# A planned order for a recurrent block beside full attention: transfers modelled alike, paired tails and products of values set beside the wide scores

## The chip, the cores and the metric

The kernel runs on one core of a Trainium2 chip. The time is the device time of one execution in microseconds (us), as a median of several executions. A core has five engines, each with its own instruction stream: PE multiplies matrices (its weight loads are listed apart as PEld), DVE and ACT work element by element and empty PE's accumulators (PSUM banks), POOL does small copies and issues transfers, and SP only issues transfers (DMA). Engines wait for one another through semaphores.

## The reference, cut to what matters

Two attention blocks read the same input `x` (2048 x 576); a gate per row mixes them.

```python
def _A_ref(x, mem0, Wq, Wk, Wv, Wo, seg_len):      # 32 heads of 128; seg_len 32, memory of 8 rows
    mem = mem0
    for s in range(n_seg):                         # 64 segments, one after the other
        h = jnp.concatenate([mem, xs], axis=1)     # 8 + 32 = 40 rows
        q, k, v = (jnp.einsum('btd,dhe->bhte', h, W) for W in (Wq, Wk, Wv))
        p = _softmax(jnp.where(mask, jnp.einsum('bhqe,bhke->bhqk', q, k) * scale, -1e9))
        o = jnp.einsum('bhte,hed->btd', jnp.einsum('bhqk,bhke->bhqe', p, v), Wo)
        mem = o[:, :M, :]                          # the memory of the next segment
        outs.append(o[:, M:, :])
def _B_ref(x, wqkv, wo):                           # plain attention, 32 heads of 18, 2048 x 2048 scores
    ...
g = _sigmoid((x * gate_w).sum(-1, keepdims=True))
return g * _A_ref(...) + (1 - g) * _B_ref(...)
```

Block A is a recurrence: segment s+1 cannot start before segment s has given its 8 memory rows. Block B has no such order, so its work can fill the time in which A waits.

## The kernel before, in words

All work is recorded as named operations (`add`, L148), each with an engine or a choice of two, a planned duration, its dependencies, a priority, buffers that it takes and gives back, and for transfers their size. `Plan.run` (L207) then places them one at a time: for every engine `choose` (L306) takes, among those that could start about first, the one with the lowest priority number, and the operation that can start earliest of all engines is placed. The result is a fixed order of instructions on each engine; on the chip each engine works through its list in that order and waits where an input is late. The planner's times are used for nothing else.

The operations that matter here, by name, segment s and half hf (16 heads each):

- `sb` (L925): one visit of block B, four concurrent matmuls of 32 rows by 128 columns ("the wide scores", mode `row`); `ex` and `ey` (ACT, L934 and L938): its exponentials; `ob` (L948): the product with the values, four matmuls of 128 rows by 32 columns (mode `col`). There are 512 visits. Scores `sb` have one buffer, exponentials `etb` two.
- `TQ0`, `TQ1`, `TV0` (L1302): the tails of two projections paired, eight matmuls of 64 by 32 (mode `quad`), three in each segment. `Q0`, `K0`, `Q1`, `K1`, `V0`, `V1` (L1312): the rest of the projections, four pieces each, mode `col`.
- `eQ`, `eK`, `eV`: copies out of PSUM (L520 on DVE, L518 on ACT); `t` (L1377): a transposing transfer on SP; `ct` (L1386): its copy into place on DVE; `ph` (L1401, L1409): A's scores; `xp`, `sm`, `rc`, `bc`, `nm`: the softmax; `po` (L1477): A's product of values, 16 matmuls of 64 by 128 (mode `tall`); `op` (L1183): the output projection; `fo` (L1525): memory rows for the next segment.
- `la` (L1018, L1022): projections of the last 8 rows of each segment, 24 units per group of 16 segments; group 0 must be ready before segment 0 can end, the others fill the recurrence. Their copies go through three buffers `vl` and are stored to `qkd` or `vld`.
- `warm` (L895): four matmuls on zeros that add nothing. The planner puts one where it foresees PE idle for more than 0.216 us, and only between the first and the last `ob` of a group of visits.

A visit may not start before a place in the recurrence has been reached (last lines of the kernel: from visit 48 on, 64 segments share the rest evenly). A planner's term `switch`, between 0.028 and 0.383, is added to the priority of any PE operation whose mode differs from the one before. `transfer` (L180) says when a transfer lands: it had one rule for the first 125 us by queue and another for later, and the weight loads of block A (`behind`, L649) were not modelled as transfers at all, only as time on POOL. `TURNS` is a table of numbers, one for each third of a segment, from which factors on the priorities of that stretch are drawn; it was found by search, offline.

Of the kernel before, what the change touches and what calls it, by code (L numbers as in the profile page):

```python
# [12 lines left out]
ACT = mybir.ActivationFunctionType  # L13
# [3 lines left out]

RANKS = [
    {
        "switch": 0.158, "near": 0.011, "early": 0.195, "wait": 0.273, "Q0": 0.964, "K0": 3.412, "Q1": 5.846,  # L20
# [5 lines left out]
        "cp": 0.432, "mn": 1.531,  # L26
    },
    {
        "switch": 0.383, "near": 0.014, "early": 0.178, "wait": 0.273, "Q0": 0.268, "K0": 3.152, "Q1": 5.787,
# [5 lines left out]
        "cp": 1.117, "mn": 1.531,  # L35
    },
    {
        "switch": 0.088, "near": 0.019, "early": 0.168, "wait": 0.273, "Q0": 0.05, "K0": 4.557, "Q1": 5.756,
# [5 lines left out]
        "mn": 1.531,  # L44
    },
    {
        "switch": 0.028, "near": 0.019, "early": 0.264, "wait": 0.014, "Q0": 0.05, "K0": 3.865, "Q1": 4.013,
# [7 lines left out]
]  # L55
RANK = dict(RANKS[0])
TURNS = [
# [16 lines left out]
]  # L74
FACTORS = (0.02, 0.1, 0.25, 0.4, 0.55, 0.7, 0.85, 1.0, 1.2, 1.5, 1.9, 2.4, 3.0, 4.0, 6.0, 10.0)
KNOBS = ("switch", "near", "early", "wait", "gap")


def mixed(turn, k):
# [35 lines left out]
class Plan:  # L115

    LANES = 8
    LATE = {"ACT": 0.055, "DVE": 0.055, "POOL": 0.06, "SP": 0.03}
    OWN = {"PE": 0.0, "ACT": 0.0, "DVE": 0.03, "POOL": 0.0, "SP": 0.0}
    OVER = {"PE": 0.0, "ACT": 0.1, "DVE": 0.08, "POOL": 0.0, "SP": 0.0}  # L120
    LAG = {"SP": 0.66, "ACT": 0.66, "POOL": 1.25}
    FAR, LANDED, RATE = 0.235, 0.025, 200.0
    EARLY = 125.0
    SWITCH = 0.103
    WARM = 0.216
    BLOCK, FETCH = 128, 3.8
    TURN = re.compile(r"(TQ0|ph0|op0)\.\d+(\.0)?$")
# [19 lines left out]

    def add(  # L148
        self, name, engs, dur, fn, deps=(), prio=5.0, mode=None, take=(), give=(), dmas=0, kb=0.0,
        pairs=4, alt=None, waits=0.0, drain=0.226, lag=None,  # L150
    ):
        op = Op(name, engs, dur, fn, deps, prio, mode, take, give)
        op.dmas, op.kb, op.lag = dmas, kb, lag
        op.pairs, op.alt, op.waits, op.drain = pairs, alt, waits, drain
        op.kind = self.kinds.setdefault(kind_of(name), len(self.kinds))
        op.seq = len(self.ops)
        self.ops.append(op)
        return op
# [21 lines left out]
    def transfer(self, op):  # L180
        step = (op.end - op.start) / op.dmas
        lag = self.LAG[op.eng] if op.lag is None else op.lag
        for j in range(op.dmas):
            issued = op.start + (j + 1) * step
            if op.end < self.EARLY and op.eng == "POOL":
                self.moved = max(self.moved, issued + 0.6) + op.kb / op.dmas / 290.0
                op.land = max(self.moved + 1.0, op.end + 2.2 + op.kb / 250.0)
            elif op.end < self.EARLY:
                self.moved = max(self.moved, issued + 0.6) + op.kb / op.dmas / 290.0
                op.land = self.moved + 0.5  # L190
            else:
                self.moved = max(self.moved, issued + lag) + op.kb / op.dmas / self.RATE
                op.land = self.moved + 0.55
            if op.eng != "POOL":
                self.lanes.append(max(op.land, self.lanes[-1]))
        self.lanes = self.lanes[-self.LANES:]
# [9 lines left out]
    def run(self):  # L206
# [96 lines left out]
                dirty = set(free)  # L303
        return order

    def choose(self, e, ops, now, mode):  # L306
        found = []
        for op in ops:
# [24 lines left out]

        def rank(f):
            op = f[1]
            switch = 0.0 if e != "PE" or mode in (op.mode, op.alt and op.alt[0]) else self.rank["switch"]
            return (self.weighed(op) + switch, op.seq)

        got = min(near, key=rank)
        urgent = [f for f in found if self.weighed(f[1]) < 1.0 and f[0] > got[0]]  # L340
        if urgent and self.weighed(got[1]) >= 1.0:
            u = min(urgent, key=lambda f: (f[0], f[1].seq))
# [19 lines left out]
def kernel(  # L362
# [286 lines left out]
    def behind(name, beat, corner, n, fn, deps, kb):  # L649

        mark = add(f"mk{name}", "DVE", 0.07, lambda e: nc.vector.memset(corner(), 0.0), [beat, *deps], prio=0.05)
        op = add(name, "POOL", 0.6 * n, fn, [mark, *deps], prio=0.15, kb=kb)
        paced.append(op)
        return op

# [577 lines left out]
    for s in range(n_seg):  # L1233
# [39 lines left out]
                        in_=xl[:, f, a, :, :].rearrange("p u (h t) -> p u h t", t=LO),  # L1273
                    )

        pl = add(f"pl{s}", "POOL", 0.95, put_l, [ll, prev.get("psh0"), prev.get("psh1")], prio=1.0, give=(("xl", ll, 0),) if s % 4 == 3 else ())

        def ld_v(e, s=s):
            for jj in range(2):
# [81 lines left out]
        for hf, ev in ((0, ev0), (1, ev1)):  # L1361
            before = [ev, prev.get(f"pso{hf}")]
            pvs.append((
                add(f"qv{hf}.{s}", "SP", 1.17, put_v(hf), before, prio=0.2, dmas=2, kb=64),
                add(f"qc{hf}.{s}", ("DVE", "POOL"), (0.585, 1.3), put_v(hf), before, prio=RANK["qc"]),
            ))

# [2 lines left out]
        for hf in range(2):  # L1370
# [3 lines left out]
            for a, ev_a in ((0, eq), (1, ek)):  # L1374
                def turn(e, hf=hf, s=s, a=a):
                    box["tt", s, a, hf] = tt = given(opened["fix"], "tt", [P, 4, P], BF16)
                    nc.sync.dma_start_transpose(out=tt[:, :, :], in_=box["tm", s, "QK"[a] + str(hf)][:, :])  # L1377

                t_ = add(
                    f"t{a}{hf}.{s}", "SP", 1.21, turn, [ev_a], prio=RANK[f"t{hf}"], take=("tt",),  # L1380
                    give=(("tm", ev_a, 0),), dmas=1, kb=128, lag=0.02,
                )

                def ct(e, hf=hf, s=s, a=a):
                    eng = nc.vector if e == "DVE" else nc.gpsimd
                    eng.tensor_copy(  # L1386
                        out=opened["qk"][:, hf, a, 0:16 * L].rearrange("p (j i t) -> p j i t", i=4, t=L)[:, :, :, 0:CT],
                        in_=box["tt", s, a, hf][:, :, :].rearrange("p i (j t) -> p j i t", t=CT),
                    )

                turned.append(add(
                    f"ct{a}{hf}.{s}", "DVE", 0.3, ct, [t_, prev.get(f"psh{hf}")],
                    prio=RANK["ct"], give=(("tt", t_, 0),),
                ))
# [380 lines left out]
```

## Time and profile before

| | us |
|---|---|
| median of 3 executions | 1467.12 (1464.38 to 1468.97) |
| the profiled execution, and its span | 1468.2, 1466.3 |
| tails of segment 0, 1 and 63 start | 129.6, 185.4, 1416.9 |
| PE busy in the span | 1346.6 |
| ACT, DVE, POOL busy | 1130.2, 785.0, 565.2 |

The span falls into three stages. In the start (to 185.4 us, where segment 1 begins) block B's projections, the first visits, the loading of A's weights and the first `la` group are done. In the recurrence (to 1416.9) segments follow at mostly 18 to 22 us each with visits in between. The tail is the last segment and the mix. A row of the timeline gives the start, the length, the engine, the line and the operation; matmuls overlap in the pipeline, so what a piece costs PE is the distance from its start to the next start, not its length.

### The profile page before, as it was taken

To read this page: it belongs to the slowest core of one execution; us is meant where nothing else is said; L and a number is where in the kernel's file an instruction comes from. 1 tells how busy PE (TensorE), PEld (TensorE's weight loads), DVE (VectorE), ACT (ScalarE), POOL (GpSimd) and SP (SyncE) were. 2 spreads that over 40 slices of the span, in tenths; PEclk is the share of its full clock that TensorE was granted. 3 is DMA by queue.
4 is the path that set the end of the run, shared out by engine and by line. 5 is a ranking of instruction groups with operands and counts; after the bars stand their busy time and mean duration, and the time that the engine had idled before them with its cause. 6 is when DMAs were issued, how large, how long until landed. Compare 5 with 4: busy or idle time off the path is not lost.

```text
span 1466.3 us, 73309 instructions
## 1 busy us (share of the span) xinstructions
PE 1346.6 (92%) x32558; PEld 685.0 (47%) x32558; DVE 785.0 (54%) x1892; ACT 1130.2 (77%) x1367; POOL 565.2 (39%) x1221
## 2 busy tenths in 40 slices
PE   8778899999999999999999999999998988899998
PEld 5335344455544444444554444555444434444445
DVE  5233465555555555545655545556555555555556
ACT  3455598888887888877888888887777877887885
POOL 8233235233542435313542316443244334442420
PEclk9899999999999999999999999999999999999999
DMA  8787434232432233232333333323234222422225
GB/s 244 217 286 244 132 65 93 56 66 54 86 65 61 55 71 87 59 69 53 84 71 71 52 71 66 84 59 79 55 73 93 52 58 48 79 55 59 50 59 185
DMA packets 245080, 130.64 MB, mean 89 GB/s; under 512 B 197583, under 2 KB 231111, under 8 KB 244763
## 3 DMA queue, kind: packets, MB, share of 16 engines
q1 hardware_dynamic: 216067, 80.47, 24.5%
q0 software_dynamic: 26560, 43.31, 11.1%
q8 instruction: 254, 4.16, 1.2%
q10 hardware_dynamic: 2136, 2.19, 0.5%
q14 instruction: 63, 0.52, 0.1%
HBM read 52.74 MB, written 31.12 MB: 57 GB/s over the span
## 4 chain that ended last, share of the span: by engine, by line
PE 58%; DMA 25%; DVE 9%; ACT 4%; issue 3%; SPq 1%; DVEq 0%; ACTq 0%; POOL 0%
DMA tt<-tm 17%; PE pvv L1312 15%; PE acc L1183 10%; PE sb L925 7%; PE ob L948 5%; PE pv L1018 4%; DVE tm L520 3%; PE pvv L1302 3%; PE pso L1477 2%; ACT etb L934 2%; DMA v_sb<-tm 2%; DMA qkd<-vl 2%; PE pq L727 2%; DMA ktd<-xn 2%; PE pv L1022 2%
## 5 line engine op out<-in xcount | busy, mean ns | idle before, releaser
L934 ACT ACTIVATE etb<-sb 128x1536 bf16<-128x1536 f32 x512 | 743.9, 1453 | 210.3 <-PE sp L925 124.2
L520 DVE CAST tm<-pvv 128x512 bf16<-128x512 f32 x336 | 230.8, 689 | 217.2 <-PE pvv L1312 203.1
L938 ACT ACTIVATE etb<-sp 128x512 bf16<-128x512 f32 x512 | 305.4, 596 | 2.8 <-PE sp L925 2.7
L1312 PEld LDWEIGHTS <-ht 128*32 128x32 bf16 x6144 | 141.1, 96 | 168.9 <-issue 74.3
L925 PE MATMUL sp<-qch,kch 32*128 32x512 bf16 x512 | 197.6, 386 | 14.6 <-DVE vl L520 5.0
L948 PE MATMUL ob<-etb,vch 128*32 128x512 bf16 x2048 | 201.3, 386 | 5.9 <-DMA vch<-vgd 5.7
L925 PE MATMUL sb<-qch,kch 32*128 32x512 bf16 x1536 | 202.2, 388 | 4.8 <-ACT etb L934 3.9
L1183 PE MATMUL acc<-wo,ot 128*32 128x288 bf16 (+1 forms) x6144 | 167.2, 250 | 5.0 <-issue 2.7
L1312 PE MATMUL pvv<-wk_m,ht 128*32 128x512 bf16 x2048 | 148.6, 382 | 0.0
L1386 DVE COPY qk<-tt 128x512 bf16<-128x512 bf16 x256 | 81.0, 320 | 126.2 <-DMA tt<-tm 124.6
L1312 PE MATMUL pvv<-wq_m,ht 128*32 128x512 bf16 x2048 | 141.7, 381 | 0.4 <-issue 0.4
L1312 PE MATMUL pvv<-wv_m,ht 128*32 128x512 bf16 x2048 | 141.0, 381 | 0.0
L1183 PEld LDWEIGHTS <-ot 128*32 128x32 bf16 x6144 | 116.3, 97 | 37.8 <-issue 16.0
L925 PEld LDWEIGHTS <-kch 32*128 32x128 bf16 x2048 | 54.1, 91 | 145.4 <-issue 136.7
L1354 POOL COPY v_sb<-tm 32x512 bf16<-32x512 bf16 x90 | 56.6, 629 | 167.1 <-DVE tm L520 139.8
L520 DVE CAST ot<-pso 128x320 bf16<-128x320 f32 x158 | 73.7, 488 | 72.7 <-PE pso L1477 69.5
L1252 POOL COPY ht<-xg 128x120 bf16<-128x120 bf16 x64 | 19.5, 305 | 207.0 <-PE pvv L1312 190.8
L1419 ACT ACTIVATE et<-psh 128x320 bf16<-128x320 f32 x128 | 56.3, 440 | 42.5 <-PE psh L1409 39.8
L844 POOL DMA_DIRECT2D otd<-stage x124 | 63.7, 520 | 50.2 <-DVE stage L991 30.3
L844 POOL DMA_DIRECT2D qch<-qtd x120 | 61.4, 519 | 54.6 <-PE sp L925 45.1
L948 PEld LDWEIGHTS <-vch 128*32 128x32 bf16 x2048 | 53.4, 95 | 60.3 <-issue 39.7
L1466 DVE TENSOR_TENSOR et<-et,prb 128x320 bf16<-128x320 bf16 x128 | 62.1, 486 | 34.4 <-PE prb L1455 29.9
(155 smaller groups left out, 2007.0 us busy)
## 6 DMA issues: line engine op xcount, KB each, us to landing
xl<-qkd SPq DMA_DIRECT2D x16, 512.0 KB
v_sb<-tm SPq DMA_DIRECT2D x256, 32.0 KB
qkd<-vl POOLq DMA_DIRECT2D x48, 128.0 KB, 2.3
wo<-in_A_Wo_dram POOLq DMA_DIRECT2D x8, 576.0 KB, 5.1
wq_m<-in_A_Wq_dram POOLq DMA_DIRECT2D x8, 512.0 KB, 6.9
vgd<-vt SPq DMA_DIRECT2D x32, 128.0 KB
wk_m<-in_A_Wk_dram POOLq DMA_DIRECT2D x8, 512.0 KB, 6.0
wv_m<-in_A_Wv_dram POOLq DMA_DIRECT2D x8, 512.0 KB, 5.9
```

The costliest lines, as they stand in the source:

```text
L520: nc.vector.tensor_copy(out=out_of(), in_=in_of())
L844: dma(out=rows_, in_=pads) if out else dma(out=pads, in_=rows_)
L925: nc.tensor.matmul(sb[:, j, :] if j < 3 else sp[:, :], lhsT=kc[r, o:o + P], rhs=qt_[r, :], start=True, stop=True, tile_position=(32 * j, 0),)
L934: nc.scalar.activation(out=etb[:, 0:3, :], in_=box["sb", gq, kb][:, :, :], func=ACT.Exp, scale=scale_b)
L938: nc.scalar.activation(out=etb[:, 3, :], in_=box["sp", gq, kb][:, :], func=ACT.Exp, scale=scale_b)
L948: nc.tensor.matmul(ob[32 * j:32 * j + 32, :], lhsT=vc[:, o + 32 * j:o + 32 * j + 32], rhs=etb[:, j, :], start=(kb == 0), stop=(kb == NKB - ...
L1018: nc.tensor.matmul(out_, lhsT=lw, rhs=rw, start=(c == 0), stop=(c == NF), skip_group_check=wide)
L1183: nc.tensor.matmul(acc[32 * q:32 * q + 32, :], lhsT=o[:, slot, t0:t0 + CT], rhs=wo[:, h, d:d + n], start=(first and s_ == (s_ % 2 if wide ...
L1312: nc.tensor.matmul(box["pvv", s, n][32 * j:32 * j + 32, :], lhsT=opened["ht", ht_i][:, c, :], rhs=rw, start=False, stop=(c == NF - 1), til ...
L1354: move(out=opened["v_sb"][64 * (j // 2):64 * (j // 2) + CT, o:o + 512], in_=tm[32 * j:32 * j + CT, :],)
L1386: eng.tensor_copy(out=opened["qk"][:, hf, a, 0:16 * L].rearrange("p (j i t) -> p j i t", i=4, t=L)[:, :, :, 0:CT], in_=box["tt", s, a, hf] ...
L1466: nc.vector.tensor_tensor(out=et[:, :], in0=et[:, :], in1=box["prb", s, hf][:, :], op=ALU.mult)
```

## The change

The planner's rules and numbers change, and the table; no operation is added, taken out or computed in another way. Apart from `warm` and the choice of engine for copies, both kernels hold the same instructions in another order.

1. Transfers: one rule for all queues, 300 GB/s with 0.8 us behind it up to 125 us, 220 GB/s and 0.55 us later; transposes and value copies get a further 0.4 and 0.3 us (`late`), and longer issue times. Weight loads are now modelled as transfers (`dmas=n`).
2. PE's choice: only modes `row`, `tall` and `quad` (`APART`) carry a term: +1.0 when PE comes from `col` or `full`, -2.0 when it comes from another of the three (`join`). Where `sb` would be taken from outside the three, a `tall` or `quad` operation that could start within 0.1 goes first (`lead`). `hold` is 0, so it does nothing.
3. ACT may be planned 0.1 us sooner behind itself (`OWN`).
4. A new `TURNS`, searched so that the orders stood up to several draws of late landings. The search is not in the kernel.

```diff
-        "switch": 0.158, "near": 0.011, "early": 0.195, "wait": 0.273, "Q0": 0.964, "K0": 3.412, "Q1": 5.846,
+        "join": 2.0, "lead": 0.1, "hold": 0.0, "switch": 1.0, "near": 0.011, "early": 0.195, "wait": 0.273, "Q0": 0.964, "K0": 3.412, "Q1": 5.846,
...
-    5930455, 8867912, 5588176, 4224530, 4462807, 3152017, 1657877, 1431486, 9342573, 3415973, 1797666, 7338397,
+    1857800, 9022675, 438981, 2889519, 430643, 9735567, 7304546, 3041551, 5216219, 6729060, 4487910, 140224, 5454171,
...
-    OWN = {"PE": 0.0, "ACT": 0.0, "DVE": 0.03, "POOL": 0.0, "SP": 0.0}
+    OWN = {"PE": 0.0, "ACT": -0.1, "DVE": 0.03, "POOL": 0.0, "SP": 0.0}
-    FAR, LANDED, RATE = 0.235, 0.025, 200.0
+    FAR, LANDED = 0.235, 0.025
+    RATES = ((300.0, 0.8), (220.0, 0.55))
+    APART = ("row", "tall", "quad")
...
+        rate, after = self.RATES[0 if op.end < self.EARLY else 1]
         for j in range(op.dmas):
             issued = op.start + (j + 1) * step
-            if op.end < self.EARLY and op.eng == "POOL":
-                self.moved = max(self.moved, issued + 0.6) + op.kb / op.dmas / 290.0
-                op.land = max(self.moved + 1.0, op.end + 2.2 + op.kb / 250.0)
-            elif op.end < self.EARLY:
-                self.moved = max(self.moved, issued + 0.6) + op.kb / op.dmas / 290.0
-                op.land = self.moved + 0.5
-            else:
-                self.moved = max(self.moved, issued + lag) + op.kb / op.dmas / self.RATE
-                op.land = self.moved + 0.55
+            self.moved = max(self.moved, issued + lag) + op.kb / op.dmas / rate
+            op.land = self.moved + after + op.late
...
-            switch = 0.0 if e != "PE" or mode in (op.mode, op.alt and op.alt[0]) else self.rank["switch"]
+            switch = 0.0
+            if e == "PE" and op.mode in self.APART and op.mode != mode:
+                switch = -self.rank["join"] if mode in self.APART else self.rank["switch"]
+            elif e == "PE" and op.goes_on:
+                switch = -self.rank["hold"]
...
+        if e == "PE" and got[1].mode == "row" and mode not in self.APART:
+            lim = got[0] + self.rank["lead"]
+            ahead = [f for f in found if f[1].mode in self.APART[1:] and f[0] <= lim and self.room(f[1], got[1], lim)]
+            if ahead:
+                return min(ahead, key=rank)
...
-        op = add(name, "POOL", 0.6 * n, fn, [mark, *deps], prio=0.15, kb=kb)
+        op = add(name, "POOL", 0.6 * n, fn, [mark, *deps], prio=0.15, dmas=n, kb=kb)
...
-                add(f"qv{hf}.{s}", "SP", 1.17, put_v(hf), before, prio=0.2, dmas=2, kb=64),
+                add(f"qv{hf}.{s}", "SP", 1.25, put_v(hf), before, prio=0.2, dmas=2, kb=64, late=0.3),
...
-                    f"t{a}{hf}.{s}", "SP", 1.21, turn, [ev_a], prio=RANK[f"t{hf}"], take=("tt",),
-                    give=(("tm", ev_a, 0),), dmas=1, kb=128, lag=0.02,
+                    f"t{a}{hf}.{s}", "SP", 1.3, turn, [ev_a], prio=RANK[f"t{hf}"], take=("tt",),
+                    give=(("tm", ev_a, 0),), dmas=1, kb=128, lag=0.02, late=0.4,
```

What this does to the order is seen at three places. Line numbers after the change are higher by 10 to 12.

**PE, segment 20, behind the tail TQ1 (tails of Q1 and K1; `ht` holds the segment's rows).** Before, the product of a visit follows the tail, and the wide scores come two pieces later:

```order
L1302 LDWEIGHTS ht_1552
L1302 MATMUL pvv<-wk_t,ht_1552 32x512
L948 LDWEIGHTS vch_118
L948 MATMUL ob<-etb,vch_118 32x512
...
L1312 LDWEIGHTS ht_1552
L1312 MATMUL pvv<-wk_m,ht_1552 32x512
```

After, the wide scores (`kch`, `qch`: keys and queries of block B) stand right behind the tail:

```order
L1314 LDWEIGHTS ht_1848
L1314 MATMUL pvv<-wk_t,ht_1848 32x512
L937 LDWEIGHTS kch_111
L937 MATMUL sb<-qch_119,kch_111 128x512
...
L937 MATMUL sp<-qch_119,kch_111 128x512
L1324 LDWEIGHTS ht_1848
L1324 MATMUL pvv<-wk_m,ht_1848 32x512
```

`sb` moved from a place between two `col` pieces to one beside a `quad` piece.

**PE, segment 20, ahead of the first half's scores `psh`, which wait for the transposes of Q0 and K0.** Before, they follow V0 with one product of block B in between:

```order
L1312 MATMUL pvv<-wv_m,ht_1552 32x512
L948 LDWEIGHTS vch_115
L948 MATMUL ob<-etb,vch_115 32x512
...
L1401 LDWEIGHTS ident
L1401 MATMUL psh<-veil,ident 32x320
```

After, that product, V1's four pieces, a visit's wide scores and another product stand between V0 and `psh` (cut to the last pieces):

```order
L937 LDWEIGHTS kch_111
L937 MATMUL sb<-qch_119,kch_111 128x512
...
L960 LDWEIGHTS vch_115
L960 MATMUL ob<-etb,vch_115 32x512
...
L1324 LDWEIGHTS ht_1848
L1324 MATMUL pvv<-wv_m,ht_1848 32x512
L1413 LDWEIGHTS ident
L1413 MATMUL psh<-veil,ident 32x320
```

`psh` moved back behind V1.

**SP, end of the start: stores of the first `la` group (`vl` to `qkd` for queries and keys, to `vld` for values) and the first transposes `tt`.** Before:

```order
L1078 DMA qkd<-vl 128x512 x3
L1128 DMA ot<-in_A_mem_dram 8x576
L1246 DMA xg<-xtd 128x5x128
L1078 DMA qkd<-vl 128x512 x5
L1377 DMA_TRANSPOSE tt<-tm 128x4x128
L1078 DMA qkd<-vl 128x512 x8
L1076 DMA vld<-vl 128x512 x2
L1259 DMA xl<-qkd 128x16x128
L1076 DMA vld<-vl 128x512 x6
L1377 DMA_TRANSPOSE tt<-tm 128x4x128 x2
```

After:

```order
L1088 DMA vld<-vl 128x512 x6
L1258 DMA xg<-xtd 128x5x128
L1140 DMA ot<-in_A_mem_dram 8x576
L1088 DMA vld<-vl 128x512 x2
L1090 DMA qkd<-vl 128x512
L1292 DMA v_sb<-vld 8x2048 x2
L1090 DMA qkd<-vl 128x512 x2
L1389 DMA_TRANSPOSE tt<-tm 128x4x128
L1090 DMA qkd<-vl 128x512 x6
L1389 DMA_TRANSPOSE tt<-tm 128x4x128
```

Values now come before keys, segment 0's first transpose comes behind all but seven of the 24 stores, and the load `xl`, which reads all of `qkd`, moved behind the last transposes. On PE segment 1 now begins after 52 visits instead of 42.

More of the change, by code (lines that the diff above doesn't have):

```diff
@@ L28 @@
     {
-        "switch": 0.383, "near": 0.014, "early": 0.178, "wait": 0.273, "Q0": 0.268, "K0": 3.152, "Q1": 5.787,
+        "join": 2.0, "lead": 0.1, "hold": 0.0, "switch": 1.0, "near": 0.014, "early": 0.178, "wait": 0.273, "Q0": 0.268, "K0": 3.152, "Q1": 5.787,
         "K1": 5.293, "V0": 6.051, "V1": 6.83, "t0": 1.463, "t1": 1.971, "ph0": 7.58, "ph1": 0.716, "sm0": 1.077,
@@ L37 @@
     {
-        "switch": 0.088, "near": 0.019, "early": 0.168, "wait": 0.273, "Q0": 0.05, "K0": 4.557, "Q1": 5.756,
+        "join": 2.0, "lead": 0.1, "hold": 0.0, "switch": 1.0, "near": 0.019, "early": 0.168, "wait": 0.273, "Q0": 0.05, "K0": 4.557, "Q1": 5.756,
         "K1": 5.718, "V0": 6.38, "V1": 7.387, "t0": 0.176, "t1": 0.309, "ph0": 7.76, "ph1": 1.41, "sm0": 0.77,
@@ L46 @@
     {
-        "switch": 0.028, "near": 0.019, "early": 0.264, "wait": 0.014, "Q0": 0.05, "K0": 3.865, "Q1": 4.013,
+        "join": 2.0, "lead": 0.1, "hold": 0.0, "switch": 1.0, "near": 0.019, "early": 0.264, "wait": 0.014, "Q0": 0.05, "K0": 3.865, "Q1": 4.013,
         "K1": 6.188, "V0": 6.84, "V1": 7.133, "t0": 0.164, "t1": 0.05, "ph0": 8.301, "ph1": 1.522, "sm0": 0.729,
@@ L57 @@
 TURNS = [
[16 rows of a table removed]
[16 rows of a table added]
 ]
 FACTORS = (0.02, 0.1, 0.25, 0.4, 0.55, 0.7, 0.85, 1.0, 1.2, 1.5, 1.9, 2.4, 3.0, 4.0, 6.0, 10.0)
-KNOBS = ("switch", "near", "early", "wait", "gap")
+KNOBS = ("switch", "near", "early", "wait", "gap", "join", "lead", "hold")
 def mixed(turn, k):
@@ L149, in add @@
         self, name, engs, dur, fn, deps=(), prio=5.0, mode=None, take=(), give=(), dmas=0, kb=0.0,
-        pairs=4, alt=None, waits=0.0, drain=0.226, lag=None,
+        pairs=4, alt=None, waits=0.0, drain=0.226, lag=None, late=0.0,
     ):
         op = Op(name, engs, dur, fn, deps, prio, mode, take, give)
-        op.dmas, op.kb, op.lag = dmas, kb, lag
+        op.dmas, op.kb, op.lag, op.late = dmas, kb, lag, late
         op.pairs, op.alt, op.waits, op.drain = pairs, alt, waits, drain
         op.kind = self.kinds.setdefault(kind_of(name), len(self.kinds))
+        op.goes_on = "PE" in op.engs and not take and bool(re.search(r"\.[1-4]$", name))
         op.seq = len(self.ops)
@@ L304, in run, with room @@
         return order
+    def room(self, a, b, at):
+        for t in set(a.take):
+            if sum(x[0] <= at for x in self.tokens[t]) < a.take.count(t) + b.take.count(t):
+                return False
+        return True
     def choose(self, e, ops, now, mode):
@@ L1274, in put_l @@
                     )
-        pl = add(f"pl{s}", "POOL", 0.95, put_l, [ll, prev.get("psh0"), prev.get("psh1")], prio=1.0, give=(("xl", ll, 0),) if s % 4 == 3 else ())
+        pl = add(f"pl{s}", "POOL", 1.2, put_l, [ll, prev.get("psh0"), prev.get("psh1")], prio=1.0, give=(("xl", ll, 0),) if s % 4 == 3 else ())
         def ld_v(e, s=s):
```

30 rows, old and new, of the table TURNS are left out of this document.

## The prediction, made before the changed kernel was run

> **What bounds the kernel now.** I read the page first, then the sums by stage, then the waits.
>
> ```profile
> PE 1346.6 (92%) x32558; PEld 685.0 (47%) x32558; DVE 785.0 (54%) x1892; ACT 1130.2 (77%) x1367; POOL 565.2 (39%) x1221
> PE 58%; DMA 25%; DVE 9%; ACT 4%; issue 3%; SPq 1%; DVEq 0%; ACTq 0%; POOL 0%
> ```
>
> PE is busy for 92% of the span, and the chain that ended last lies on PE for 58% and on transfers for 25%. So PE sets the time, with transfers next. By stage (the start, the recurrence, the tail; then three stretches of the start):
>
> ```profile
> core 0: us, PE busy (x) PEld busy (x) DVE busy (x) ACT busy (x) POOL busy (x), PEclk, DMA share, GB/s
> 0.00:185.40 185.40, 153.46 (x1606) 78.38 (x1606) 74.10 (x190) 91.32 (x103) 78.30 (x182) 0.94 0.72 222
> 185.40:1416.90 1231.50, 1149.14 (x30220) 579.88 (x30220) 679.77 (x1632) 1008.46 (x1228) 483.95 (x1033) 0.99 0.32 66
> 1416.90:1466.30 49.40, 43.98 (x732) 26.78 (x732) 31.14 (x70) 30.38 (x37) 2.95 (x6) 1.00 0.53 162
> 30.00:60.00 30.00, 23.97 (x218) 11.45 (x217) 9.94 (x25) 12.17 (x14) 11.68 (x30) 0.83 0.77 241
> 95.00:130.00 35.00, 29.64 (x308) 17.87 (x307) 13.45 (x36) 21.14 (x23) 18.90 (x33) 0.91 0.95 315
> 130.00:160.00 30.00, 24.17 (x301) 14.89 (x294) 10.71 (x24) 15.30 (x17) 6.55 (x10) 0.93 0.65 200
> ```
>
> PE idles 185.40 - 153.46 = 31.9 us in the start and 1231.50 - 1149.14 = 82.4 us in the recurrence. In the start the DMA engines are 72% busy, 95% in one stretch: data come late there. In the recurrence they are 32% busy, and what PE waits for is the latency of single steps. Those waits, longest PE ones first (total, times, longest), with two that stand behind them:
>
> ```profile
> PE psh L1409 <- DVE qk L1386: 20.6, 27, 1.9
> PE psh L1401 <- DVE tm L520: 8.7, 10, 1.5
> PE prb L1455 <- DVE rq L1447: 8.6, 14, 1.4
> ...
> DVE qk L1386 <- DMA tt<-tm: 124.6, 110, 3.4
> ACT etb L934 <- PE sp L925: 124.2, 202, 7.0
> ```
>
> The largest is A's scores `psh` waiting for the transposed queries and keys. ACT mostly waits for PE, not the other way round.
>
> **The change part by part.** As no operation is added apart from `warm`, every term is a matter of order. The sum is made against the profiled execution, 1468.2 us, which is 1.1 above the median of 1467.1.
>
> *Changes of mode.* Their price is read from starts on PE:
>
> ```profile
> 703.83 0.39 PE L925 MATMUL sb<-qch,kch 32*128 32x512 bf16 x3
> ...
> 704.16 0.40 PE L948 MATMUL ob<-etb,vch 128*32 128x512 bf16 x4
> 704.38 0.40 PE L1022 MATMUL pv<-xL,wk_m 128*32 128x128 bf16 x16
> ...
> 704.77 0.37 PE L1477 MATMUL pso<-et,v_sb 64*128 64x40 bf16 x16
> 705.07 0.40 PE L1018 MATMUL pv<-xL,wk_m 128*128 128x128 bf16 x4
> ...
> 708.04 0.37 PE L1477 MATMUL pso<-et,v_sb 64*128 64x40 bf16 x16
> 708.34 0.39 PE L925 MATMUL sb<-qch,kch 32*128 32x512 bf16 x3
> ```
>
> Both visits' pieces stream 512 columns. The product, followed by its own mode, takes 704.38 - 704.16 = 0.22; the wide scores, followed by another mode, 704.16 - 703.83 = 0.33. So leaving a mode costs about 0.105. Entering is the mirror of it:
>
> ```profile
> 186.83 0.39 PE L1312 MATMUL pvv<-wk_m,ht 128*32 128x512 bf16 x4
> 187.16 0.39 PE L925 MATMUL sb<-qch,kch 32*128 32x512 bf16 x3
> ...
> 187.48 0.40 PE L1312 MATMUL pvv<-wk_m,ht 128*32 128x512 bf16 x4
> ```
>
> A `col` piece ahead of wide scores costs 0.33 instead of 0.22. A product of values `pso` takes 0.30 to the next piece whether wide scores follow (708.34 - 708.04) or a full matmul (705.07 - 704.77). So two of the three apart modes side by side still pay the change between them; side by side there are three changes where apart there are four. Counted over both orders, wide scores stand beside a `pso` 46 times before and 68 after, beside a tail 48 and 66 times, and all changes of mode go from 1679 to 1631. 48 x 0.105 = **-5.0 us**. It is on the path, since PE is. Wide scores right behind a tail (25 times after, never before) have no row; if that change cost nothing the term would be -5.0 - 25 x 0.105 = -7.6, and if it cost double, -2.4. I take the value of the row nearest to it, `pso` to `sb`.
>
> [...] Were the three one class, the groups of them (738 before, 696 after) would count, two changes each: 42 x 2 x 0.105 = 8.8 instead of 5.0.
>
> *Ten visits moved into the start.* Segment 1 begins after 52 visits instead of 42. A visit costs PE 0.22 + 0.33 + 0.11 = 0.66, so the recurrence loses ten of them, **-6.6 us**, and ten pairs of exponentials on ACT. The start gets them, and 36 blocks of `warm` where it had 1.
>
> ```profile
> L934 ACT ACTIVATE etb<-sb 128x1536 bf16<-128x1536 f32 x512 | 743.9, 1453 | 210.3 <-PE sp L925 124.2
> L938 ACT ACTIVATE etb<-sp 128x512 bf16<-128x512 f32 x512 | 305.4, 596 | 2.8 <-PE sp L925 2.7
> ...
> L895 PE MATMUL ob<-ident,nil 128*32 128x512 bf16 x452 | 40.9, 391 | 0.0
> ```
>
> *The start itself.* What hides 6.6 us of visits and 35 x 0.22 = 7.7 us of `warm` there is PE's 31.9 us of idle time. Without that cover the start is 14.3 us longer. The other limit is ACT: one visit takes it 1.45 + 0.60 = 2.05.
>
> ```profile
> 115.80 1.54 PE pv L1018 x25
> ...
> 185.42 0.40 PE pvv L1302 x8
> ```
>
> From the first `la` unit (115.8) to segment 1 (185.4) the kernel takes 69.6 us for 21 visits. After the change 33 visits lie on that stretch, 33 x 2.05 = 67.7 at the least; so it could stay as long as it is, or grow. In front of it the order now knows that weight loads use the DMA engines, and spreads two kinds of stores over two sets of buffers, which can shorten 115.8. SP's queue speaks for and against: the first transpose stands behind 17 of the 24 stores instead of 8, and `xl`, without which A's scores of segment 0 cannot start, behind all transposes of that segment. I take **0**, between -10 (a third of the idle time) and +14.3.
>
> *More work ahead of the transposes.* Priced at distances like those above, with `warm` left out, the PE work between the last piece of K0 and the first half's `psh` is 5.04 us in the mean of 62 segments before and 5.60 after; for K1 and the second half 5.36 and 5.89. The latency to cover is a cast of 0.7, the transfer and a copy of 0.3; the transfer itself, out of the chain:
>
> ```profile
> 698.40 3.42 DMA tt<-tm
> ...
> 718.40 3.99 DMA tt<-tm
> ```
>
> That is 4.4 to 5.0 in all, so the cover before was just short of it in many segments and is now mostly above. 27 waits x 0.5 us = 13.5 at the most by the one row of 20.6; **-10 us**, between 0 (transfers are as late as PE is early) and -20 (all of it).
>
> *Less work behind the wide scores.* What was moved ahead of the transposes is taken from elsewhere. From the start of a visit's scores to its product ACT needs 2.05 and two releases, about 2.45. The order holds less than that in 41 visits before and in 88 after (`warm` left out, visits 45 to 508); the shortfalls add up to 15.0 and 27.7 us. The softmax steps lose too: `psh` to `sm` goes from 1.32 to 1.20 in the first half, `sm` to `bc` from 0.71 to 0.63. Behind a waiting `ob` everything on PE queues, the next segment's steps included. **+10 us**, between 0 (the delays before them, which remain, give the time) and +18 (12.7 and 5 for the softmax).
>
> *`warm` in the recurrence* goes from 100 to 113 blocks; they stand where the order foresees idle time and cost nothing there, or 13 x 0.22 = 2.9 if it is wrong. The new planned durations (SP's, `late`, `OWN`) act through the order alone. The tail has the same 35 changes of mode: 0.
>
> Sum: 1468.2 - 5.0 - 6.6 + 0 - 10 + 10 = 1456.6; less 1.1 for the median, 1455.5, or **1456**.
>
> **The rivals.**
>
> *The start grows (slower).* If visits between the first `la` unit and segment 1 go at the recurrence's mean spacing rather than ACT's least, the ten come on top. The wide scores alone, by stage:
>
> ```profile
> 185.40:1416.90 1231.50, 193.39 (x1836) 48.56 (x1836) 0.99 0.32 66
> ```
>
> 1836 matmuls are 459 visits in 1231.5 us, 2.68 each. 33 x 2.68 = 88.4 instead of 69.6, +18.8: **1475**. For it: 17 stores ahead of the first transpose, `xl` last, and 36 blocks of `warm`, which say that the order itself foresees idle time there. Against it: the recurrence's spacing holds A's work, of which the start has one segment. It decides from a spacing of about 2.6.
>
> *Nothing gained from the cover (no change).* Transposes stay late, because what PE does sooner delays the casts on DVE, and the scores' product waits as priced: 1456 + 10 = **1466**. For it: the transfers' time moves between 3.42 and 3.99 in neighbouring segments, more than the 0.5 gained.
>
> *The start shrinks (clearly faster).* The old order knew nothing of the weights' transfers. If a third of the idle time of the start goes and the transposes give all they can: 1456 - 10 - 10 = **1436**. For it: PEclk of 0.83 and 0.91 in stretches with waits, so that a filled wait also gives back clock. [...]
>
> *The change does not do what it says* is excluded by the order: the neighbours of the wide scores were counted there.
>
> **How the numbers follow.** The forecast (1449 to 1462) gets 0.40, the start that shrinks 0.15, no gain 0.23, the start that grows 0.22. A measurement of this kernel can tell about 0.3%, 4.4 us, from no change. Faster than 1462.7: 0.40 + 0.15 = 0.55; within: 0.23; slower than 1471.5: 0.22. The range runs from about the middle of the shrinking start's case to just past that of the growing one, which leaves out some 0.18: 1437 to 1476.
>
> **What would show it.** Right: segment 1 starting near 185 us; `psh` waiting for `qk` about 10 us in all instead of 20.6; `ob` waiting for `etb` more than now; wide scores behind a tail at 0.33 from start to start. Wrong: segment 1 at 200 or at 170; waits on `qk` as before; the recurrence, from segment 1 to segment 63, longer than 1231 - 6.6 - 5.

## The result and the profile after

The changed kernel takes **1402.13 us** (median of 4 runs, 1399.96 to 1405.71) beside 1466.32 for the kernel before on the same chip (4 runs, 1464.38 to 1468.97): a ratio of 0.9563, 95% interval 0.9538 to 0.9589. It is 64 us faster. The prediction had the direction, but a sixth of the size (-11), and its range ended at 1437.

The profiled execution took 1405.7 us. Its page first, busy times and the chain that ended last, by engine and then by line:

```profile
span 1403.9 us, 73319 instructions
PE 1336.8 (95%) x32599; PEld 692.1 (49%) x32608; DVE 790.1 (56%) x1902; ACT 1122.5 (80%) x1361; POOL 563.7 (40%) x1217
PE 50%; DMA 11%; DVE 7%; ACT 4%; issue 3%; POOL 1%; SPq 0%; DVEq 0%; ACTq 0%; POOLq 0%
PE pvv L1324 15%; DMA tt<-tm 10%; PE acc L1195 9%; PE sb L937 6%; PE ob L960 5%; PE pvv L1314 3%; ACT etb L946 2%; PE pso L1489 2%; DVE tm L532 2%; PE pv L1030 2%; DMA v_sb<-tm 1%; PE prb L1467 1%; PE po L1710 1%; DVE qk L1398 1%; PE psh L1421 1%
```

PE's busy time fell by 10 us only; the rest is waiting that went. The chain says where, but its shares can't be set beside those of before as they stand: after the change they sum to 76%, since the chain can be followed back only to 323 us, while that of before (25% on transfers) covers the whole span. The chain of before, by line:

```profile
DMA tt<-tm 17%; PE pvv L1312 15%; PE acc L1183 10%; PE sb L925 7%; PE ob L948 5%; PE pv L1018 4%; DVE tm L520 3%; PE pvv L1302 3%; PE pso L1477 2%; ACT etb L934 2%; DMA v_sb<-tm 2%; DMA qkd<-vl 2%; PE pq L727 2%; DMA ktd<-xn 2%; PE pv L1022 2%
```

Taken over the same segments in both, from the first tail of segment 9 to that of segment 63, transfers had 243.7 of 1071.7 us before (23%) and have 158.2 of 1031.0 after (15%). Almost all of the fall is one of them, the transposes `tt<-tm`: 214.1 us before, 135.5 after.

The windows of the changed kernel, by stage, then two stretches of the start:

```profile
core 0: us, PE busy (x) PEld busy (x) DVE busy (x) ACT busy (x) POOL busy (x), PEclk, DMA share, GB/s
0.00:170.70 170.70, 158.78 (x1832) 83.23 (x1841) 74.92 (x192) 110.96 (x125) 82.99 (x190) 0.99 0.77 242
170.70:1356.70 1186.00, 1135.30 (x30063) 583.42 (x30063) 682.23 (x1636) 983.98 (x1204) 477.73 (x1022) 1.00 0.32 69
1356.70:1403.90 47.20, 42.68 (x704) 25.47 (x704) 32.95 (x74) 27.55 (x33) 2.95 (x6) 0.99 0.57 170
30.00:60.00 30.00, 28.94 (x259) 14.49 (x260) 14.10 (x36) 15.02 (x17) 15.52 (x35) 1.00 0.93 299
60.00:90.50 30.50, 30.30 (x222) 14.19 (x221) 16.18 (x43) 20.73 (x23) 18.19 (x31) 1.00 1.02 368
```

The start is 14.7 us shorter, the recurrence 45.5, the tail 2.2. PE idles 170.70 - 158.78 = 11.9 us in the start (31.9 before) and 1186.00 - 1135.30 = 50.7 in the recurrence (82.4 before). In the start the transfers now run almost without gaps in the two stretches where the weights come, at a DMA share of 0.93 and 1.02 and 299 and 368 GB/s. Rows chosen from its waits (us in total, times, longest):

```profile
ACT etb L946 <- PE sp L937: 171.1, 253, 12.9
DVE qk L1398 <- DMA tt<-tm: 62.0, 72, 3.0
PE psh L1421 <- DVE qk L1398: 10.6, 21, 2.3
PE sb L937 <- ACT etb L946: 8.8, 18, 1.6
PE prb L1467 <- DVE rq L1459: 7.6, 17, 1.2
PE sp L937 <- DVE tm L532: 2.5, 5, 0.7
PE psh L1413 <- DVE tm L532: 1.4, 3, 0.7
PE ob L960 <- ACT etb L946: 1.2, 1, 1.2
```

Three rows of before that the prediction did not show:

```profile
PE pvv L1302 <- DVE tm L520: 4.9, 6, 1.5
PE sp L925 <- DVE tm L520: 4.9, 8, 0.8
PE sb L925 <- ACT etb L934: 3.9, 12, 0.5
```

`psh` behind `qk` is halved, as predicted. But a larger fall is on DVE: it stood still ahead of the copies `ct` (`qk<-tt`) for 124.6 us, now for 62.0. Behind it most of PE's own waits on DVE's casts went: the first half's `psh` on `tm` from 8.7 to 1.4, `sp` from 4.9 to 2.5, and `pvv`, 4.9 before, is gone from the list. The wait that the prediction had set against all this, `ob` on `etb`, came once; in its neighbourhood the scores `sb`, which have one buffer, wait longer for the exponentials, 8.8 instead of 3.9.

### The profile page after: what moved, and what is told of

Same layout as the page of the kernel before. It is cut to its first block, busy times and chain, and to the rows that moved or that the text cites. A ratio compares the mean times of both kernels' runs of the same rounds, so it can differ in the third digit from the quotient of the medians.

```text
span 1403.9 us, 73319 instructions
## 1 busy us (share of the span) xinstructions
PE 1336.8 (95%) x32599; PEld 692.1 (49%) x32608; DVE 790.1 (56%) x1902; ACT 1122.5 (80%) x1361; POOL 563.7 (40%) x1217
## 3 DMA queue, kind: packets, MB, share of 16 engines
q1 hardware_dynamic: 216067, 80.47, 25.7%
## 4 chain that ended last, share of the span: by engine, by line
PE 50%; DMA 11%; DVE 7%; ACT 4%; issue 3%; POOL 1%; SPq 0%; DVEq 0%; ACTq 0%; POOLq 0%
PE pvv L1324 15%; DMA tt<-tm 10%; PE acc L1195 9%; PE sb L937 6%; PE ob L960 5%; PE pvv L1314 3%; ACT etb L946 2%; PE pso L1489 2%; DVE tm L532 2%; PE pv L1030 2%; DMA v_sb<-tm 1%; PE prb L1467 1%; PE po L1710 1%; DVE qk L1398 1%; PE psh L1421 1%
## 5 line engine op out<-in xcount | busy, mean ns | idle before, releaser
L532 DVE CAST tm<-pvv 128x512 bf16<-128x512 f32 x342 | 235.6, 690 | 244.7 <-PE pvv L1324 237.3
L1324 PEld LDWEIGHTS <-ht 128*32 128x32 bf16 x6144 | 145.4, 96 | 167.8 <-issue 62.4
L1195 PE MATMUL acc<-wo,ot 128*32 128x288 bf16 (+1 forms) x6144 | 164.3, 248 | 4.9 <-issue 3.1
L1324 PE MATMUL pvv<-wk_m,ht 128*32 128x512 bf16 x2048 | 143.0, 382 | 0.0
L1264 POOL COPY ht<-xg 128x120 bf16<-128x120 bf16 x64 | 20.4, 320 | 237.6 <-PE pvv L1324 234.6
L532 DVE CAST ot<-pso 128x320 bf16<-128x320 f32 x152 | 70.6, 485 | 49.4 <-PE pso L1489 47.2
L1283 POOL COPY qk<-xl 128x128 bf16<-128x128 bf16 x256 | 67.7, 301 | 42.8 <-PE psh L1421 34.9
```

Of the source, the lines that this page charges most:

```text
L532: nc.vector.tensor_copy(out=out_of(), in_=in_of())
L1195: nc.tensor.matmul(acc[32 * q:32 * q + 32, :], lhsT=o[:, slot, t0:t0 + CT], rhs=wo[:, h, d:d + n], start=(first and s_ == (s_ % 2 if wide ...
L1283: nc.gpsimd.tensor_copy(out=opened["qk"][:, f, a, 0:16 * L].rearrange("p (u h t) -> p u h t", h=4, t=L)[:, :, :, CT:L], in_=xl[:, f, a, :, ...
L1324: nc.tensor.matmul(box["pvv", s, n][32 * j:32 * j + 32, :], lhsT=opened["ht", ht_i][:, c, :], rhs=rw, start=False, stop=(c == NF - 1), til ...
```

## The experiments

**Theories.** (1) DVE's queue: a `ct` that waits for a late transpose holds up everything behind it on DVE (casts that empty PSUM, the next transposes' inputs, reciprocals); the new order gives it cover, and that is most of the recurrence's gain. (2) Modes: fewer changes on PE, worth more than priced. (3) Clock: less idle time and a higher granted clock (0.985 before, 0.995 after in the profiled executions). A second question is which rule of the planner did it. Each experiment has runs of the kernel before on the same chip beside it; deltas to the changed kernel are differences of ratios times 1466.

**e1: the changed kernel, each `ct` one place earlier on DVE.** PE's order stays as it is.

```diff
-        for op in self.run():
+        for op in self.sooner(self.run(), 1):    # 210 of 256 ct move ahead of the DVE operation before them,
+                                                 # none ahead of what it depends on
```

> The kernel after, with each copy `ct` of a transpose moved one place earlier in DVE's order (never ahead of the issue of its transpose). Nothing else moves. Theory A (DVE stands still behind copies whose transposes have not landed, and everything queued behind them, PSUM copies above all, makes PE wait): DVE's waits for tt rise from 62 to about 100 us, and the time from 1402 to 1420 or more. Theory B (only the work on PE ahead of psh matters, as the prediction had it): psh gets its input no later, so the time stays within 5 us of 1402.

Measured: 1454.52 us (6 runs, 1440.16 to 1457.35), ratio 0.9886 [0.9838, 0.9934]: +47 us to the changed kernel. The profile's recurrence takes 1230.2 us; before's took 1231.5. Its waits:

```profile
DVE qk L1416 <- DMA tt<-tm: 177.5, 148, 3.8
PE pvv L1332 <- DVE tm L550: 17.2, 18, 2.4
PE prb L1485 <- DVE rq L1477: 15.5, 23, 1.7
PE sp L955 <- DVE tm L550: 12.0, 15, 1.7
PE psh L1439 <- DVE qk L1416: 5.1, 7, 1.5
```

One place on DVE, and nearly the whole gain of the recurrence is gone. Note the last row: `psh` waits *less* for `qk` than in the changed kernel (5.1 instead of 10.6). The loss is in what stands behind the copy, not in who uses it: PE waits for DVE's casts `tm` and its reciprocals `rq`. Segment 28 in both kernels shows how, on DVE's timeline. First e1, whose memory rows `ht` come at 714.72; a row gives start, length, line, operation, and in brackets the idle time ahead of it and its cause (the segment's first cast stands ahead of these rows):

```profile
717.77 0.69 DVE L550 CAST tm<-pvv 128x512 bf16<-128x512 f32 x1 [0.67 <-PE pvv L1342]
719.80 0.29 DVE L1416 COPY qk<-tt 128x512 bf16<-128x512 bf16 x1 [1.34 <-DMA tt<-tm]
720.00 0.68 DVE L550 CAST tm<-pvv 128x512 bf16<-128x512 f32 x1
722.76 0.29 DVE L1416 COPY qk<-tt 128x512 bf16<-128x512 bf16 x1 [2.08 <-DMA tt<-tm]
722.97 1.28 DVE L550 CAST tm<-pvv 128x512 bf16<-128x512 f32 x2
...
726.04 0.35 DVE L1416 COPY qk<-tt 128x512 bf16<-128x512 bf16 x1 [1.01 <-DMA tt<-tm]
```

The changed kernel, where `ht` comes at 690.61:

```profile
693.66 0.69 DVE L532 CAST tm<-pvv 128x512 bf16<-128x512 f32 x1 [0.67 <-PE pvv L1324]
695.58 0.69 DVE L532 CAST tm<-pvv 128x512 bf16<-128x512 f32 x1 [1.23 <-PE pvv L1324]
696.19 0.28 DVE L1398 COPY qk<-tt 128x512 bf16<-128x512 bf16 x1
696.66 0.69 DVE L532 CAST tm<-pvv 128x512 bf16<-128x512 f32 x1 [0.19 <-PE pvv L1324]
698.09 0.29 DVE L1398 COPY qk<-tt 128x512 bf16<-128x512 bf16 x1 [0.73 <-DMA tt<-tm]
...
701.25 0.44 DVE L1398 COPY qk<-tt 128x512 bf16<-128x512 bf16 x1 [0.38 <-DMA tt<-tm]
```

The fourth cast, input of the fourth transpose, starts 696.66 - 690.61 = 6.05 us after `ht` in the changed kernel. In e1 it stands behind a copy that idles 2.08, and starts at 8.25. In this segment the last copy starts 0.7 us later (11.32 against 10.64): a late copy makes the next transpose late, which makes the next copy late. That is one segment, and not the mean. Over the 62 segments of the recurrence the last copy starts 12.6 us later in sum (0.20 each, between -2.4 and +3.3), and from the last copy to the last product of values `pso` e1 takes 31.3 us more. So most of the 44.2 us by which the two recurrences differ comes behind the last copy. Before's segments are longer than the changed kernel's at the same two places: 12.0 us in sum up to the last copy, 32.5 from it to `pso`.

**e2: the kernel before, each `ct` one place later; e10: the changed kernel, the same.** The other direction of e1.

```diff
-        for op in self.run():
+        for op in self.later(self.run(), 1):     # past one DVE operation, where no user of the copy
+                                                 # and no taker of its buffer tt comes in between
```

> The kernel before, with each copy `ct` of a transpose moved one place later in DVE's order where the order leaves room ahead of its user (about 165 of 256). Theory A: DVE's waits for tt fall from 125 to about 90 us and the time from 1466 to 1450 or less. Theory B: psh gets its input as late or later, so the time is 1466 to 1475.

> The kernel after with each copy ct one place later in DVE's order where there is room ahead of its user (143 of 256 move). Theory A alone (DVE standing still is all that counts): DVE's waits for tt fall below 62 and the time below 1400. If both ends of the copy count, as the same edit of the kernel before suggests: DVE's waits fall, psh waits more than 10.6 us, and the time is 1405 to 1430.

Measured: e2 1480.92 us (10 runs, 1470.10 to 1487.97), ratio 1.0096 [1.0064, 1.0129], 158 of 256 copies moved; e10 1415.96 us (4 runs), 0.9651 [0.9607, 0.9694], 143 moved, +13 to the changed kernel. e2's waits (its profile is of 1473.04 us, one of its shorter executions), then two rows of e10's:

```profile
DVE tm L535 <- DMA tt<-tm: 51.2, 29, 2.8
DVE qk L1401 <- DMA tt<-tm: 41.0, 47, 2.7
PE psh L1424 <- DVE qk L1401: 41.2, 55, 2.4
...
PE psh L1436 <- DVE qk L1413: 25.9, 42, 2.4
DVE qk L1413 <- DMA tt<-tm: 37.6, 43, 2.6
```

In e2 the standing before the copies went from 124.6 to 41.0, and the kernel is slower. Now `psh` waits twice as long for `qk` as in the kernel before, and casts wait for transposes to give `tm` back. In e10 the standing fell from 62.0 to 37.6, and `psh` waits 25.9 instead of 10.6. So theory 1 in its simple form (standing time on DVE is what counts) falls. In the changed kernel a copy has a best place with a loss on both sides, and in the kernel before moving the copies alone does not bring the gain.

PE's idle time in the recurrence, summed by what ended it, shows both sides (from the first tail of segment 1 to that of segment 63, us):

| | all | DVE's casts `tm` | reciprocals `rq` | copies `qk` | transfers `v_sb` |
|---|---|---|---|---|---|
| before | 82.4 | 18.1 | 13.3 | 20.4 | 5.3 |
| changed kernel | 50.7 | 4.3 | 8.5 | 10.6 | 1.7 |
| e1, copies earlier | 86.3 | 35.3 | 16.2 | 5.1 | 3.5 |
| e10, copies later | 59.5 | 2.4 | 6.8 | 25.7 | 1.7 |
| e2, before with copies later | 87.8 | 15.0 | 4.5 | 40.9 | 2.4 |

A copy that comes early costs casts and reciprocals, one that comes late costs its reader. From before to the changed kernel the four columns behind the first fell, by 32.0 us together. That PE's order, which gives the later copies cover, made this possible is read from these rows; no run put the new order of PE beside the old order of DVE.

**e3: the changed kernel, 53 wide scores taken from beside a tail or product of values, one PE piece later; e9: a control, 53 other wide scores one piece later, without a change of mode.**

```diff
-        for op in self.run():
+        for op in self.parted(self.run()):       # e3: (quad|tall), sb, (col|full) -> (quad|tall), (col|full), sb
+        for op in self.shifted(self.run()):      # e9: plain, sb, plain -> plain, plain, sb
```

> The kernel after, with the wide scores that stand right behind a paired tail or a product of values moved one piece of PE later, so that a col or full piece stands between them: 1677 changes of mode instead of 1631, about those of the kernel before (1679). If a change costs 0.105 us, as the rows of the kernel before say, +46 x 0.105 = 4.8: about 1407. If setting them side by side is what made the kernel faster, 1430 or more.

> Control for the run that parted the wide scores from tails and products: in the kernel after, 53 other wide scores, with col or full pieces on both sides, stand one piece of PE later. As many moves, none of the changes of mode (1631). If the 18 us of the parted kernel came from the changes of mode, 1400 to 1405. If they came from the exponentials that start later, 1415 to 1422.

Measured: e3 1420.31 us, 0.9685 [0.9650, 0.9720], changes of mode 1631 to 1677; e9 1410.14 us, 0.9622 [0.9572, 0.9673]. By the medians, moving scores at all costs 9 us, though e9's interval touches the changed kernel's (0.9538 to 0.9589). Parting them costs 0.0063 x 1466 = 9 more, 0.2 for each of 46 changes where 0.105 was priced (4.8). The intervals of e3 and e9 overlap, so that this is twice the price isn't shown; at most (0.9720 - 0.9572) x 1466 = 22 us would fit them. That bounds theory 2.

The direct price is in the changed kernel's timeline, where wide scores stand right behind a tail, which never happened before:

```profile
462.99 0.39 PE L1314 MATMUL pvv<-wk_t,ht 64*32 64x512 bf16 x1
463.31 0.40 PE L1324 MATMUL pvv<-wk_m,ht 128*32 128x512 bf16 x4
...
465.81 0.41 PE L1314 MATMUL pvv<-wv_t,ht 64*32 64x512 bf16 x8
466.15 0.39 PE L937 MATMUL sb<-qch,kch 32*128 32x512 bf16 x3
...
466.48 0.40 PE L960 MATMUL ob<-etb,vch 128*32 128x512 bf16 x4
```

From a tail's first start, 465.81, to the scores' are 0.34 us (25 such places, all 0.341 to 0.343). To a `col` piece it is the same: the tail of which the first row shows the last matmul began at 462.97, and 463.31 - 462.97 = 0.34.

**e4: the changed kernel without its 154 `warm` blocks** (work on zeros, left out).

```diff
-        for op in self.run():
+        for op in (o for o in self.run() if o.name != "warm"):
```

> The kernel after without its 154 blocks of warm (matmuls on zeros, no part of the result). If they only fill time in which PE waits: 1397 to 1405, with the granted clock down by 0.01 or less. If they hold the clock up and that is where the gain came from (0.985 before, 0.995 after): 1415 or more and a clock near 0.98.

Measured: 1403.63 us (4 runs), 0.9566 [0.9531, 0.9602]: no difference to 0.9563. The mean granted clock of its profile is 0.984, that of the changed kernel's 0.995, in the same time. Theory 3 falls: a lower clock while PE has less to do cost nothing here.

**e5 to e8, e11, e12: which rule of the planner.** Each is one planner with a table `TURNS` of its own, found by a short search: for each third of a segment the best of 100 draws, judged by the idle time that the planner foresees on PE six thirds later (e7: 40 draws, eight thirds). So the table is not the change's, and no draws of late landings enter. Each planner was tried with one table. e5 is the old planner, e8 the new one. The edits against e5, by the parts of the change:

```diff
 e6: + rates and landing rule of `transfer`, `late`, issue times, `dmas=n` for weights, `OWN`
 e7: + `join`, `lead`, `APART`
 e8: + both
 e11 (later rule alone):  +                op.land = self.moved + 0.55 + op.late
                          + the issue times 1.25, 1.3, 1.2; late=0.3 and late=0.4
 e12 (start alone):       +            if op.end < self.EARLY:
                          +                self.moved = max(self.moved, issued + lag) + op.kb / op.dmas / 300.0
                          +                op.land = self.moved + 0.8
                          + dmas=n for the weight loads
```

> The planner before, with a table found by a short search of ours (for each third of a segment the best of 100 draws, judged by PE's planned waste six thirds later). Its own plan ends at 1406.6, that of the kernel before at 1319.9 and that of the kernel after at 1336.1; on the chip these take 1466 and 1402, that is 146 and 66 more than planned. Theory M (the rules for transfers make plans that the chip keeps): this one, with the old rules, ends about 140 above its plan, near 1545. Theory J (wide scores beside tails and products): the same, since it has neither. If the new table was merely a luckier draw, all four of this batch end at a like distance from their plans.

> The planner after with the old rule for PE's choice (old switch terms, no join, no lead), new rules for transfers, and a table by the same search; planned 1396.5. Theory M: about 66 above its plan, near 1465. Theory J: about 140 above, near 1535.

> The planner after with the old rules for transfers, issue times and ACT, and the new rule for PE's choice; a table by the same search (40 draws, eight thirds ahead); planned 1420.9. Theory M: about 140 above, near 1560. Theory J: about 66 above, near 1487.

> The planner after as it is, with a table by the same search (100 draws, six thirds ahead); planned 1407.3. Theories M and J: about 66 above, near 1473. If the search over late landings that made the new table gave the gain and not the rules, 1510 or more.

> The planner before, plus the late landings of transposes and value copies (0.4 and 0.3) and the longer issue times alone; a table by the same search (100 draws, six thirds ahead), planned 1407.1. Old rules ended 122 above their plans, new ones 72 to 79. If most of the 45 to 50 us are made in the recurrence by the late landings: about 90 above, near 1497. If they are made in the start: about 120 above, near 1527.

> The planner before, plus the new rule for transfers up to 125 us and the weight loads as transfers alone; a table by the same search, planned 1408.1. The counterpart of the run with late landings alone: about 100 above its plan, near 1508, if the start gives about 20; about 75 above, near 1483, if it gives nearly all.

Measured, with the end that each planner itself gave its order (which no chip has run), and how far the chip missed it. DVE's standing and PE's idle time in the start (to segment 1) are from each profile:

| | median us | planned end | missed by | `qk` on `tt` | PE idle in start |
|---|---|---|---|---|---|
| before | 1466.3 | 1319.9 | 146 | 124.6 | 31.9 |
| e5 old planner | 1528.25 | 1406.6 | 122 | 102.3 | 32.4 |
| e7 old + PE's choice | 1543.55 | 1420.9 | 123 | 110.6 | 41.9 |
| e12 old + start | 1504.13 | 1408.1 | 96 | 106.3 | 13.8 |
| e11 old + late landings | 1509.74 | 1407.1 | 103 | 49.9 | 31.9 |
| e6 old + all transfers | 1475.21 | 1396.5 | 79 | 65.4 | 15.5 |
| e8 new planner | 1479.27 | 1407.3 | 72 | 66.2 | 22.7 |
| changed kernel | 1402.1 | 1336.1 | 66 | 62.0 | 11.9 |

The rows of two of them: e11's wait on DVE, in which the late landings show,

```profile
DVE qk L1369 <- DMA tt<-tm: 49.9, 60, 2.0
```

and e12's window of the start, where 173.00 - 159.18 = 13.8 us are idle on PE:

```profile
0.00:173.00 173.00, 159.18 (x1802) 82.23 (x1802) 77.93 (x197) 105.54 (x117) 80.50 (x186) 0.97 0.75 239
```

The two halves of the transfer rules part cleanly. Wherever late landings are modelled, DVE stands 50 to 66 us, otherwise 102 to 125. Wherever the start is, PE idles 12 to 23 us there, otherwise 32 to 42. At nearly equal planned ends (1406.6 to 1408.1) late landings bring 18 us by the medians, the start rules 24, the whole change of the planner 49. The first two are not clear of noise: the ratios of e11 [1.0224, 1.0363] and e12 [1.0184, 1.0326] overlap that of e5 [1.0284, 1.0567]; that of e8 [1.0040, 1.0101] does not. The sizes are of one table each (2 runs for e5, e7, e11 and e12, 8 for e6 and e8), and another table can shift them: before and e5 are one planner and miss by 146 and 122. The waits, of one profile each, part without an exception and are the firmer ground. PE's choice, the part with the tails beside the wide scores, brings nothing that stands out of this: e7 misses its plan as e5 does, and e6 [1.0029, 1.0082] and e8 can't be told apart.

## Why the prediction was right in sign and wrong in size

- **Changes of mode and ten visits (-5.0, -6.6): in line with the sum.** PE's busy time in the recurrence fell by 1149.14 - 1135.30 = 13.8 for the -11.6 priced. That is no proof of the two terms: e1 has the changed kernel's order on PE, and its busy time there is 1143.94, 8.6 more. The one change without a row costs the 0.34 of its neighbour, so the three modes are not one class. Where one `col` piece follows another, the same timeline has 0.22 (463.97 to 464.19).
- **The start (0): wrong in size; it was -14.7.** Segment 1 began at 170.7, which the prediction had named as a sign of being wrong. The rival that shrank the start had the right reason (weight loads known to the order) and too low a limit, a third of the idle time: 20.0 of 31.9 us went. e12, with the start's rules alone, has 19 us less idle time there than e5. The rival that grew it fell: from the first `la` unit (90.5) to segment 1 are 80.2 us for 33 visits, 2.43 each, below the 2.6 from which it decided. That stretch did grow, by 10.6 us, but it began 25.3 earlier.
- **More work ahead of the transposes (-10): the step that failed.** For its own wait it was right: `psh` on `qk` fell from 20.6 to 10.6. There is luck in that, since the place of the copies on DVE alone moves this wait between 5.1 (e1) and 25.9 (e10), and the price left that place out. Above all the prediction priced the cover by PE's distance to `psh` only. The row that it had quoted beside it, DVE standing 124.6 us before the same copies, was read as standing "behind" PE's wait and given no term. What is queued on DVE behind such a copy waits with it, as the cast behind the 2.08 us in e1 does, and it feeds PE's banks, the softmax and the next transposes. PE's idle time in the recurrence fell by 31.7 us, where the sum had -10 and +10: 9.8 of it is the wait that was priced, and 13.8 on casts, 4.8 on reciprocals and 3.6 on `v_sb` had no term. e1 shows that this place has that size (+44.2 in the recurrence, with `psh` waiting less); e2 shows that it isn't had by moving copies alone. How much of it is DVE's order and how much PE's stays open.
- **Less work behind the wide scores (+10): did not come.** `ob` waited for `etb` once, 1.2 us, and `sb` for the exponentials 4.9 us more than before. In the softmax, for which 5 of the +18 stood, PE's wait for reciprocals fell (13.3 to 8.5). Every shortfall in the order was counted as lost; why almost none was is open.
- **`warm` (nothing): right**, by e4. **Clock** as a gain of filled waits: not shown, since e4 has the lower clock and the same time. The clock's mean reading was 0.995 with the blocks and 0.984 without. In 30 to 60 us it was 0.83 before, with 30.00 - 23.97 = 6.0 us idle on PE, and 1.00 after, with 30.00 - 28.94 = 1.1; but in 60 to 90.5 us before it was 1.00 with 30.50 - 24.08 = 6.4 idle. That the clock gave time back there no run shows.
- **"No gain from the cover"** fell: `psh` waits 10.6 us for `qk`, where it waited 20.6.

Open: of the 80 us by which the change brings chip and plan closer (146 to 66), the planner's rules account for about 43 to 50 (122 to 79 or 72). Before's longer searched table misses its plan by 24 more than e5's, while the change's does not miss by more than e8's. Whether the judging of tables over draws of late landings does that, or the truer rules leave a search less to exploit, wasn't tried.

## What to carry to other kernels

Where an engine works in order, price a wait by everything that is queued behind it, on that engine and on those that it feeds, not by the one reader of the late value; a row with a large idle time on an engine that "has time" is a term of the sum. A planner that lands transfers too early builds its whole order on the error: with tables of the same short search the chip missed the old rules' plan by 122 us and the new rules' by 72. Compare the planned end with the chip's, and look at the resource that misses most. A copy that waits on a transfer has a best place in its queue: one place earlier cost 47 us here, one later 13.

## What the runs showed that was not expected

- One place in DVE's queue for 210 copies, with PE's order untouched, is worth 3% of the kernel.
- In 60 to 90.5 us the transfers moved 368 GB/s at a DMA share of 1.02, beside 315 at 0.95 in the fullest stretch before. Scaled to a share of 1, the whole start gives 222 / 0.72 = 308 GB/s before and 242 / 0.77 = 314 after: the old order left the DMA engines idle rather than slow.
- A mean granted clock of 0.984 (without `warm`) and one of 0.995 gave 1403.6 and 1402.1 us: here the mean clock was lower where PE's waits were longer (its three largest sums 15.1, 14.1 and 12.5 us without the blocks, 10.6, 8.8 and 7.6 with them), and the time did not change.
